# A Fourier convolution with two expert layers on one core: the beginning in another order, with weight pieces on POOL and chunk 3's sums later

## The chip, the core and the metric

The kernel runs on one core of a Trainium2 chip. The metric is the device time of one execution in microseconds, the median of several runs. The engines are called PE (matrix products), DVE and ACT (elementwise), POOL (a second, slower elementwise engine, which also issues DMAs here) and SP (issues DMAs). Each engine works through its own instructions strictly in their order and waits where an operand isn't there.

## The reference, cut to what matters

```python
X = np.fft.rfft(x, axis=1)                       # x: 8 batches, 3072 points, 256 channels
y = np.fft.irfft(X * (filt_r + 1j * filt_i), n=3072, axis=1)
t = y.reshape(8 * 3072, 256)                     # 24576 tokens
h = np.maximum(np.maximum(t @ w1, t @ w2), t @ w3)    # w1, w2, w3: 256 x 768
t = h @ w_out                                    # first expert layer; w_out: 768 x 256
h = t @ w_in                                     # second expert layer, 1024 wide
solu = h * softmax(h)
out = layer_norm(solu) * g_ln @ w_out2
```

## The kernel before, in words

The channels of a batch make two chunks of 128, so there are 16 chunks, numbered batch by batch. A transform of 3072 points is split into 24 times 128. Chunks 0 to 3 (the first two batches) get their 24-point sums on PE, in quarters of 8 small products (`quarter`, L696 to L708 before the change), and after the transform back their parts go to DRAM (`parts_i`). They are read back turned (`turn_in`, into the tile `z`) and get their last sums on PE against the constant `im` (`turn_first`). The later chunks do their 24-point sums on DVE.

`first_batch` does chunks 0 and 1 before everything else, as eight units, a unit being a chunk and one of four groups of frequencies, in the order of `UNITS`. A unit has three stages. `fwd_in`: ACT multiplies the slab `S` by twiddles, DVE sums the products to `U`. `middle`: four PE products of `U` with the constant `dfull`, then on DVE two products with the filter `F` (tiles `Y` and `M2`, read from PSUM) and two sums. `inv_out`: four PE products of `Y`, which ACT copies to `v0` and writes to DRAM. For six units a tile is 384 columns wide, for two (the group `(0, 3)` and `(1, 3)`) 512.

Then the first expert layer begins. Tokens come in tiles of 512, six to a batch, and `moe(i)` is one step of one tile and 128 of the 768 hidden columns, six steps to a tile. `up` makes 12 PE products; ACT and DVE take the maximum and split it into a high and a low part (`hh`, `hl`). `down` is the six products with `w_out`, two steps behind `up` (`LD = 2`), so PE asks for a step's `hl` only after the `up` of the two next steps. `xT` makes the input of a tile. The kernel uses w1 - w3 and w2 - w3 and adds x times A, A being w3 times w_out, at a tile's end.

The weights arrive as float64 bits. `moe_weights` takes them in 12 pieces of 128 by 512 (`PIECES`; for each third of the hidden columns first w3, then w1, w2, w_out). A piece takes five DVE and two ACT operations to become float32 (`from_f64`), then up to three more on DVE and a cast on ACT for the difference, the high and the low part. Ten pieces (`EARLY`) stand among the units, the others behind them. At the end `moe_weights` makes A.

The transforms of chunks 2 to 15 run beside the expert layer. They are one long generator (`fft_stream`), and after each step the main loop lets it advance until its counted DVE work reaches a line set by the step's number (`PACE`, `LEAD`). A scheduler fixes every engine's order when the program is built; `issue_after(x)` keeps instructions behind `x` on x's engine.

Of the kernel before, what the change touches and what calls it, by code (L numbers as in the profile page):

```python
# [10 lines left out]
F32 = mybir.dt.float32  # L11
# [127 lines left out]
def kernel(ctx: ExitStack, tc: tile.TileContext, x0, xr, ff, tw, dft, first_f, first_i,  # L139
# [17 lines left out]
    make_identity(nc, ident)  # L157

# [56 lines left out]
    EARLY = 10  # L215

    def moe_weights():

        raws = yp.tile([P, 3, 1024], I32, tag="s4", name="raws")
        for i, (q, j) in enumerate(PIECES):  # L220
# [13 lines left out]
            with tc.issue_after(GATE[0]) if i >= EARLY else nullcontext():  # L234
                v = from_f64(raw, e, w3f[:, :, fs] if j == 2 else None, nc.vector)
# [4 lines left out]
                if j < 2:  # L240
                    nc.vector.tensor_tensor(v, v, w3f[:, :, fs], op=ALU.subtract)
                nc.scalar.copy(hi, v)
                o = nc.vector.tensor_tensor(lo, v, hi, op=ALU.subtract)
# [3 lines left out]
        pw = [bank() for c in range(2)]  # L247
        for f in range(NF):
# [7 lines left out]
            for c in range(2):  # L256
                cs = slice(c * P, (c + 1) * P)
                nc.tensor.matmul(pw[c][:, :D], th[:, cs], wo_h[:, f], start=f == 0, stop=False)
                nc.tensor.matmul(pw[c][:, :D], tl[:, cs], wo_h[:, f], start=False, stop=False)
                nc.tensor.matmul(pw[c][:, :D], th[:, cs], wo_l[:, f], start=False, stop=f == NF - 1)  # L260
        for c in range(2):
            nc.scalar.copy(a_h[:, c], pw[c][:, :D])
            nc.vector.tensor_tensor(a_l[:, c], pw[c][:, :D], a_h[:, c], op=ALU.subtract)
# [207 lines left out]
    def middle(ch, g):  # L471
# [19 lines left out]
        nc.sync.dma_start(F.rearrange("p r w -> p (r w)"), ff[dc, :, foff:foff + 2 * W])  # L491
# [47 lines left out]
    def inv_out(ch, g):  # L539
# [22 lines left out]
        if ch < 2 * BF:  # L562
# [10 lines left out]
            nc.scalar.dma_start(parts_i[ch][6 * g:6 * g + 6].rearrange("s n d -> n s d"), v)  # L573
# [82 lines left out]
    def fft_stream():  # L656

        last = 2 * B - 1
        yield from groups(2)
# [10 lines left out]
    FZ, SUMS = {}, {}  # L670
# [7 lines left out]
    def first_batch():  # L678
# [16 lines left out]
        def quarter(ch, q, eng):  # L695
            if ch < 2:  # L696
                xs = xa[ch][0][:NT, 8 * q:8 * q + 8] if q < 3 else xa[ch][1][:NT]
            else:
                r = 12 + 8 * (q % 2)
                xs = scr0[:NT, r:r + 8]  # L700
                nc.sync.dma_start(xs, x0[ch, :, 8 * q:8 * q + 8])
            pf = pairbank(0)
# [6 lines left out]

        busy(4)  # L710
        for ch in range(2):
            S[ch] = slab(ch)
            for q in range(4):
                e = quarter(ch, q, nc.scalar if q % 2 and not ch else nc.vector)
                if (ch, q) == (1, 1):
                    behind = e.ins
            for _ in fwd_in(*UNITS[ch]):
                pass
        with tc.issue_after(behind):
            for _ in range(2):  # L720
                next(wgen)
        behind = e.ins
        S[2], S[3] = slab(2), slab(3)
        for i, u in enumerate(UNITS):
# [4 lines left out]
            for q in {0: (0, 1), 2: (2,), 4: (3,)}.get(i, ()):  # L729
                quarter(2, q, nc.scalar)  # L730
            with tc.issue_after(behind):
# [3 lines left out]
                for _ in inv_out(*u):  # L735
                    pass
                if i in (1, 2, 3, 5, 6):
                    next(wgen)
            if i == 4:
                FZ["z"] = fc.tile([P, 2, 2, 6, P], F32, tag="s0", name="z0")  # L740
                turn_in(0, 0, (0,))
            if i == 6:
                FZ["im"] = fc.tile([P, NG, NT], F32, tag="s1", name="im")
                nc.sync.dma_start(FZ["im"][:NT], first_i)
                nc.sync.dma_start(df, dft[:, 0:4])
        GATE.append(behind)
        turn_in(0, 0, (1,))
        with tc.issue_after(FZ["mm"]):
            for q in range(4):
                quarter(3, q, nc.scalar)  # L750
        with tc.issue_after(behind):
            for _ in range(3):
                next(wgen)
# [463 lines left out]
```

## Time and profile before

| | |
|---|---|
| median of 3 runs | 2709.89 us (2709.13 to 2710.82) |
| the profiled execution | 2711.81 us |
| its span in the trace | 2710.0 us |
| PE busy | 2671.7 us, 99% of the span |
| DVE, ACT, POOL busy | 2154.2, 1579.1, 909.1 us |
| mean granted TensorE clock | 0.994 of full speed |

The profile is of one execution; the times in the rows are its own. Busy time of PE counts a product that runs at half the clock as fully busy, so idle time and the granted clock have to be read together. The span is 1.8 us shorter than the profiled execution's own time, and that is 1.9 us above the median.

### The profile page before, as it was taken

The page shows a single profiled execution, that of the slowest core. Times are in us where ns is not written, and L with a number is a line of the kernel's source. Part 1 is how long each engine was busy: PE and PEld are TensorE (multiplying, and loading weights), DVE is VectorE, ACT ScalarE, POOL GpSimd, SP SyncE. Part 2 cuts the span into 40 slices and gives each one's busy share as a digit, 9 for nine tenths or more (in the row PEclk, how much of TensorE's full clock was granted, in tenths as well). Part 3 has the DMA queues.
Part 4 walks back from the last instruction along what each step waited for, and adds up shares of the span by engine and source line. Part 5 has one row for each costly group of instructions (what it writes and reads, how often), then busy time and mean ns, then how long its engine had stood idle before and what let it go on. Part 6 is the DMA issues. An engine that isn't in the chain of part 4 may idle for free.

```text
span 2710.0 us, 38330 instructions
## 1 busy us (share of the span) xinstructions
PE 2671.7 (99%) x12368; PEld 2178.7 (80%) x12368; DVE 2154.2 (79%) x3539; ACT 1579.1 (58%) x3000; POOL 909.1 (34%) x1311
## 2 busy tenths in 40 slices
PE   8899999999999999999999999999999999999999
PEld 6677777877777777777887888888888888888888
DVE  6787787699998999989755447878877887888875
ACT  5544554455555555546344335777777777777775
POOL 0011111011111111121010003767667666767675
PEclk9899999999999999999999999999999999999999
DMA  7633223133223223232123104555555555555553
GB/s 218 189 112 115 75 77 87 63 82 119 68 68 124 74 75 111 75 104 75 47 79 89 37 24 107 150 144 147 149 145 143 140 142 141 141 147 144 142 129 89
DMA packets 168937, 297.17 MB, mean 110 GB/s; under 512 B 33600, under 2 KB 99136, under 8 KB 167104
## 3 DMA queue, kind: packets, MB, share of 16 engines
q1 hardware_dynamic: 113024, 232.77, 32.4%
q10 hardware_dynamic: 54416, 57.24, 6.6%
q0 software_dynamic: 1296, 4.72, 0.5%
q8 instruction: 97, 1.59, 0.3%
q14 instruction: 104, 0.85, 0.1%
HBM read 97.20 MB, written 56.62 MB: 57 GB/s over the span
## 4 chain that ended last, share of the span: by engine, by line
PE 80%; DVE 11%; DMA 4%; issue 2%; SPq 1%; ACT 1%; POOL 1%; DVEq 0%; ACTq 0%; POOLq 0%
PE h L822 21%; PE h L1005 19%; PE p L1074 13%; PE p L1076 7%; PE pf L433 5%; PE o L851 4%; PE o L843 4%; PE o L844 3%; PE o L842 3%; DVE scr L285 2%; DVE S L285 1%; DVE M L285 1%; DMA swap<-M 1%; SPq L782 1%; DVE h L827 1%
## 5 line engine op out<-in xcount | busy, mean ns | idle before, releaser
L1067 POOL TENSOR_TENSOR sl<-zt,sh 128x1024 fp32r<-128x1024 f32 x188 | 453.8, 2414 | 117.5 <-ACT sh L1066 107.5
L1074 PE MATMUL p<-V,sh 128*128 128x512 f32 x1536 | 380.4, 389 | 0.0
L285 POOL TENSOR_TENSOR M<-M,M 128x384 f32<-128x384 f32 (+1 forms) x112 | 153.2, 1389 | 666.2 <-DVE M L285 525.7
L830 ACT CAST hh<-h 128x512 fp32r<-128x512 f32 x288 | 170.6, 592 | 329.9 <-DVE h L827 314.4
L1016 DVE SCALAR_TENSOR_TENSOR sp<-h,e 128x1024 f32<-128x1024 f32 x192 | 234.1, 1219 | 153.1 <-ACT e L1014 151.2
L1074 PEld LDWEIGHTS p<-V,sh 128*128 128x128 f32 x1536 | 287.2, 188 | 59.3
L1014 ACT ACTIVATE e<-h,sm 128x1024 f32<-128x1024 f32 x192 | 213.8, 1114 | 110.3 <-DVE sm L1012 70.4
L825 ACT ACTIVATE hm<-h 128x512 f32<-128x512 f32 x288 | 174.4, 607 | 170.8 <-PE h L822 170.1
L1012 DVE TENSOR_REDUCE sm<-h 128x1 f32<-128x1024 f32 x192 | 231.6, 1206 | 47.8 <-PE h L1005 46.8
L827 DVE TENSOR_TENSOR h<-hm,h 128x512 f32<-128x512 f32 x288 | 197.6, 686 | 79.5 <-PE h L822 77.2
L1066 ACT CAST sh<-zt 128x1024 fp32r<-128x1024 f32 x188 | 196.6, 1047 | 106.8 <-PE p L1074 92.9
L1018 ACT ACTIVATE e<-sp,sm 128x1024 f32<-128x1024 f32 x192 | 220.5, 1148 | 54.4 <-DVE sm L1020 46.5
L1005 PE MATMUL h<-wih,x2h 128*128 128x512 f32 x768 | 242.9, 392 | 1.2 <-ACT xo L854 1.2
L831 DVE TENSOR_TENSOR hl<-h,hh 128x512 fp32r<-128x512 f32 x288 | 196.3, 683 | 58.8 <-ACT hh L830 58.7
L1005 PE MATMUL h<-wih,x2l 128*128 128x512 f32 x768 | 242.1, 391 | 0.0
L843 PE MATMUL o<-hl,woh 128*128 128x512 f32 x576 | 234.9, 408 | 6.4 <-DVE hl L831 6.1
L1005 PE MATMUL h<-wil,x2h 128*128 128x512 f32 x768 | 238.5, 390 | 0.0
L1033 DVE STREAM_TRANSPOSE yt<-sp 128x1024 f32<-128x1024 f32 x188 | 231.5, 1231 | 4.1
L842 PE MATMUL o<-hh,woh 128*128 128x512 f32 x576 | 232.4, 404 | 0.8 <-ACT hh L830 0.8
L844 PE MATMUL o<-hh,wol 128*128 128x512 f32 x576 | 225.9, 392 | 0.0
L1076 PEld LDWEIGHTS p<-V,sl 128*128 128x128 f32 x1536 | 209.7, 190 | 14.9
L1076 PE MATMUL p<-V,sl 128*128 128x256 f32 x1536 | 214.9, 282 | 0.0
(175 smaller groups left out, 5693.2 us busy)
## 6 DMA issues: line engine op xcount, KB each, us to landing
zt<-yt SPq DMA_DIRECT2D x752, 128.0 KB, 2.6
x<-xo SPq DMA_DIRECT2D x96, 256.0 KB, 2.2
x<-x ACTq DMA_DIRECT2D x48, 512.0 KB, 3.6
F<-in_ff_dram SPq DMA_DIRECT2D x48, 384.0 KB, 3.5
S<-in_xr_dram SPq DMA_DIRECT2D x12, 1536.0 KB, 7.2
out_dram<-ob ACTq DMA_DIRECT2D x144, 128.0 KB, 2.3
zt<-yt SPq DMA_DIRECT2D x560, 32.0 KB, 1.8
F<-in_ff_dram SPq DMA_DIRECT2D x16, 512.0 KB, 3.8
```

Source lines behind the costliest of these rows:

```text
L285: return eng.tensor_tensor(o, a, b, op=op)
L822: nc.tensor.matmul(ph[j], wt[:, c, f * P:(f + 1) * P], xt[:, c], start=i == 0, stop=i == 5)
L842: nc.tensor.matmul(po[m], wo_h[:, f, cs], hh, start=f == 0, stop=False)
L843: nc.tensor.matmul(po[m], wo_h[:, f, cs], hl, start=False, stop=False)
L844: nc.tensor.matmul(po[m], wo_l[:, f, cs], hh, start=False, stop=False)
L1005: nc.tensor.matmul(h[:, fs], xt[:, c, ts], wt[:, c, fs], start=n == 0, stop=n == 5)
L1012: nc.vector.tensor_reduce(sm[:, 0:1], h, axis=AX.X, op=ALU.max, negate=True)
L1016: nc.vector.scalar_tensor_tensor(sp, h, 1.0, e, op0=ALU.mult, op1=ALU.mult, accum_out=sm[:, 2:3])
L1033: nc.vector.transpose(out=YT[g][:, :, t].rearrange("p j c k -> p c j k"), in_=sp.rearrange("p (c j k) -> p c j k", c=NF2, j=4))
L1067: nc.gpsimd.tensor_tensor(lv, z, hv, op=ALU.subtract)
L1074: nc.tensor.matmul(p, sh[:, c], V2[:, c], start=c == 0, stop=False)
L1076: nc.tensor.matmul(p[:, :D], sl[:, c], V2[:, c, :D], start=False, stop=c == NF2 - 1)
```

## The change

The line numbers of the changed kernel are higher by 8 in the transforms, by 17 in `quarter` and by 45 or 46 in the expert layer. It does the following.

- The first ten steps take tiles 0 and 1 in turn for the first third of the hidden columns (`BOTH`), and then tile 0, then tile 1. Tile 0 gets its own accumulator (`ob`), whose banks go to the transforms after step 9.
- Six instead of ten weight pieces stand among the units, starting at the third, and of these six the last product, the difference, the cast and the low part go from DVE and ACT to POOL. Six pieces stay behind the units.
- Unit 0's and unit 1's `fwd_in` come before chunk 1's quarters. Chunk 2's quarters come at units 5, 6 and 7 and behind the last unit. Chunk 3's four quarters go into the transform stream (`later`).
- Each unit's parts are read back alone, for tiles 0 and 1, four units later. The last unit's are written in eight pieces by ACT and SP and read back in two halves of the rows.
- The transform stream starts behind step 9 instead of step 4, and its line is five steps later.
- A's two halves share one PSUM bank, which a product with zeros opens.

```diff
-    EARLY = 10
+    EARLY = 6
...
             with tc.issue_after(GATE[0]) if i >= EARLY else nullcontext():
-                v = from_f64(raw, e, w3f[:, :, fs] if j == 2 else None, nc.vector)
+                eng = nc.gpsimd if i < EARLY else nc.vector
+                v = from_f64(raw, e, w3f[:, :, fs] if j == 2 else None, eng)
...
-                nc.scalar.copy(hi, v)
-                o = nc.vector.tensor_tensor(lo, v, hi, op=ALU.subtract)
+                if i < EARLY:
+                    nc.gpsimd.tensor_copy(hi, v)
+                else:
+                    nc.scalar.copy(hi, v)
+                o = eng.tensor_tensor(lo, v, hi, op=ALU.subtract)
...
+            if (ch, g) == UNITS[-1]:
+                for r in (slice(0, 12), slice(12, NG)):
+                    for i in range(NI):
+                        queue = nc.scalar if i % 2 else nc.sync
+                        queue.dma_start(dst[NG * i:NG * (i + 1)][r], v[NG * i:NG * (i + 1)][r])
+                    if not r.start:
+                        turn_in(0, 0, ch, g)
+                        turn_in(0, 1, ch, g)
...
+            if i == 0:
+                quarter(1, 3, nc.vector, first(7))
...
-                for _ in inv_out(*u):
+                for _ in inv_out(*u) if i < 7 else ():
                     pass
-                if i in (1, 2, 3, 5, 6):
-                    next(wgen)
+                if i >= 2 and i < 2 + EARLY:
+                    with tc.issue_after(FL[UNITS[1]]):
+                        next(wgen)
+            if i in (5, 6, 7):
+                quarter(2, i - 5, nc.scalar, x2[:NT, 8 * (i - 5):8 * (i - 5) + 8])
...
+            if i >= 4:
+                turn_in(0, 0, *UNITS[i - 4])
+                turn_in(0, 1, *UNITS[i - 4])
...
         with tc.issue_after(FZ["mm"]):
+            quarter(2, 3, nc.scalar, x23)
...
+        def later():
             for q in range(4):
-                quarter(3, q, nc.scalar)
-        with tc.issue_after(behind):
-            for _ in range(3):
-                next(wgen)
...
+                quarter(3, q, nc.scalar, xs[q])
+                yield
...
-    steps = [(b, tg, f) for b in range(B) for tg in range(TG) for f in range(NF)]
+    BOTH = [(0, 0), (0, 1), (1, 0), (1, 1)] + [(tg, f) for tg in range(2) for f in range(2, NF)]
+    steps = [(0, tg, f) for tg, f in BOTH]
+    steps += [(b, tg, f) for b in range(B) for tg in range(TG) for f in range(NF) if b or tg > 1]
...
-        if i < 4:
-
+        if i < NB:
             continue
...
-        while cost[0] - c0 < (i + 1) * PACE + LEAD * min(1.0, i / RAMP) and idle < 12:
+        while cost[0] - c0 < (i - 4) * PACE + LEAD * min(1.0, (i - 5) / RAMP) and idle < 12:
```

The first place is the first unit on PE. `U` with `dfull` is the unit's first product, `f24` marks a quarter, `Y` the product back. Before:

```order
L705 MATMUL pf_257<-f24_154,xq_164 128x24x4 x8
L433 MATMUL pf_305<-U_216,dfull_137 128x384 x4
L705 MATMUL pf_317<-f24_154,scr0_142 128x24x4 x8
L705 MATMUL pf_328<-f24_154,scr0_142 128x24x4 x8
L433 MATMUL pf_348<-Y_310,dfull_137 128x384
L433 MATMUL pf_358<-U_267,dfull_137 128x384 x4
L433 MATMUL pf_348<-Y_310,dfull_137 128x384 x3
```

With the change:

```order
L722 MATMUL pf_259<-f24_156,xa_165 128x24x4 x8
L441 MATMUL pf_273<-U_219,dfull_139 128x384
L722 MATMUL pf_284<-f24_156,xq_166 128x24x4 x6
L441 MATMUL pf_273<-U_219,dfull_139 128x384 x3
L722 MATMUL pf_284<-f24_156,xq_166 128x24x4 x2
L441 MATMUL pf_304<-Y_278,dfull_139 128x384
L441 MATMUL pf_314<-U_229,dfull_139 128x384 x4
L441 MATMUL pf_304<-Y_278,dfull_139 128x384 x3
```

Two quarters of chunk 2 are gone from between the unit's products and the first product back; only the rest of chunk 1's last quarter stands there.

The second place is the end of `first_batch` on PE, up to the first tile of the expert layer (`h` from `im` and `z`). Before:

```order
L433 MATMUL pf_614<-Y_608,dfull_137 128x384 x3
L433 MATMUL pf_651<-Y_645,dfull_137 128x384 x4
L705 MATMUL pf_661<-f24_154,scr0_142 128x24x4 x8
L705 MATMUL pf_672<-f24_154,scr0_142 128x24x4 x8
L705 MATMUL pf_683<-f24_154,scr0_142 128x24x4 x8
L705 MATMUL pf_694<-f24_154,scr0_142 128x24x4 x8
L767 MATMUL h_751<-im_635,z0_555 128x96 x5
```

With the change:

```order
L722 MATMUL pf_541<-f24_156,x2_269 128x24x4 x8
L441 MATMUL pf_555<-U_460,dfull_139 128x384
L441 MATMUL pf_521<-Y_505,dfull_139 128x384 x3
L441 MATMUL pf_555<-U_460,dfull_139 128x384 x3
L441 MATMUL pf_566<-Y_560,dfull_139 128x384
L722 MATMUL pf_584<-f24_156,x2_269 128x24x4 x8
L441 MATMUL pf_598<-U_511,dfull_139 128x384
L441 MATMUL pf_566<-Y_560,dfull_139 128x384 x3
L441 MATMUL pf_598<-U_511,dfull_139 128x384 x3
L722 MATMUL pf_622<-f24_156,x2_269 128x24x4 x8
L441 MATMUL pf_642<-Y_603,dfull_139 128x384 x4
L722 MATMUL pf_659<-f24_156,scr0_144 128x24x4 x8
```

Chunk 3's four quarters are gone from behind the last product back, and one quarter of chunk 2 (`pf_659`) stands there, right ahead of the first tile; the other quarters of chunk 2 stand among the last units, where `Y_560` follows at once on the products of `U_460` that it depends on.

The third place is DVE between the low parts `hl` of two steps in a row of the expert layer, steps 12 and 13 of the changed kernel, counted from 0. `scr` and `S` are the sums of 24 points of chunk 4, `Z`, `M1` and `U` belong to chunk 2:

```order
L876 TENSOR_TENSOR hl_1552<-h_1535,hh_1551 128x512
L293 TENSOR_TENSOR scr_1346<-S_1344 128x1536 x2
L293 TENSOR_TENSOR scr_1346<-scr_1346 128x768
L293 TENSOR_TENSOR S_1344<-scr_1346 128x768
L293 TENSOR_TENSOR S_1344<-scr_1346 128x384 x2
L873 TENSOR_TENSOR h_1619<-hm_1632,h_1619 128x512
L293 TENSOR_TENSOR scr_1346<-scr_1346 128x384 x2
L297 SCALAR_TENSOR_TENSOR Z_1232<-pf_1227,tws_137,M2_1233 128x768
L297 SCALAR_TENSOR_TENSOR S_1344<-scr_1346 128x768 x2
L293 TENSOR_TENSOR U_1251<-U_1251,T_1252 128x384 x2
L293 TENSOR_TENSOR M1_1240<-Z_1232,F_1225 128x768
L876 TENSOR_TENSOR hl_1636<-h_1619,hh_1635 128x512
```

Before the change such sums of chunk 4 stood between the steps 4 to 8; they have moved about eight steps back, into steps that had little DVE work.

## Rows read from the trace of the kernel before

**Rows 1.** The page: busy us of each engine, share of the span, instructions.
```profile
PE 2671.7 (99%) x12368; PEld 2178.7 (80%) x12368; DVE 2154.2 (79%) x3539; ACT 1579.1 (58%) x3000; POOL 909.1 (34%) x1311
```
**Rows 2.** Windows: stretch, length, busy us (instructions) by engine, PE clock, DMA share, GB/s.
```profile
0.00:89.23 89.23, 76.94 (x330) 49.84 (x330) 64.32 (x111) 49.24 (x106) 6.39 (x15) 0.95 0.80 223
89.23:105.23 16.00, 10.03 (x65) 9.44 (x63) 9.57 (x19) 8.87 (x13) 1.45 (x2) 0.71 0.66 184
105.23:115.00 9.77, 9.77 (x36) 8.69 (x37) 9.66 (x19) 6.45 (x13) 0.00 (x0) 0.56 0.23 60
115.00:150.00 35.00, 33.08 (x159) 25.51 (x158) 24.04 (x37) 21.32 (x52) 6.54 (x7) 1.00 0.58 175
150.00:170.00 20.00, 15.46 (x64) 11.17 (x63) 19.01 (x26) 7.79 (x17) 3.18 (x2) 0.91 0.39 113
170.00:1600.00 1430.00, 1421.42 (x6130) 1131.78 (x6129) 1166.09 (x1730) 712.84 (x1582) 167.64 (x137) 1.00 0.28 81
1600.00:2710.00 1110.00, 1104.97 (x5595) 942.31 (x5593) 861.49 (x1601) 772.63 (x1221) 723.88 (x1148) 1.00 0.52 134
```
**Rows 3.** PE's timeline: start, us, instruction, records; in brackets idle before it and releaser.
```profile
25.79 3.85 PE L705 MATMUL pf<-f,scr 96*128 96x96 f32 x32 [1.53 <-DMA scr<-in_x_dram]
...
31.13 2.74 PE L433 MATMUL pf<-U,dfull 128*128 128x384 f32 x8
33.71 2.10 PE L433 MATMUL pf<-Y,dfull 128*128 128x384 f32 x6
...
52.34 2.01 PE L433 MATMUL pf<-Y,dfull 128*128 128x512 f32 x2 [2.41 <-DVE Y L285]
...
83.77 5.46 PE L433 MATMUL pf<-Y,dfull 128*128 128x384 f32 x8 [3.02 <-DVE Y L285]
...
105.23 5.33 PE L767 MATMUL h<-im,z 96*128 96x96 f32 x24 [0.89 <-ACT S L708]
...
169.48 0.40 PE L844 MATMUL o<-hh,wol 128*128 128x512 f32 x1
169.71 0.39 PE L842 MATMUL o<-hh,woh 128*128 128x512 f32 x1
```
**Rows 4.** DVE's timeline in one unit, with weight operations between.
```profile
40.29 0.95 DVE L285 TENSOR_TENSOR Y<-pf,F 128x768 f32<-128x768 f32 x1
41.16 0.95 DVE L285 TENSOR_TENSOR M<-pf,F 128x768 f32<-128x768 f32 x1
42.02 0.42 DVE L201 TENSOR_SCALAR raws<-raws 128x512 int32<-128x512 int32 x1
42.35 1.02 DVE L285 TENSOR_TENSOR Y<-Y,M 128x384 f32<-128x384 f32 x2
43.29 0.68 DVE L285 TENSOR_TENSOR U<-U,T 128x512 f32<-128x512 f32 x1
43.90 0.42 DVE L197 TENSOR_SCALAR we<-raws 128x512 int32<-128x512 int32 x1
```
**Rows 5.** ACT's timeline: the last unit's copy.
```profile
89.27 0.80 ACT L566 COPY v<-pf 128x768 f32<-128x768 f32 x1 [2.20 <-PE pf L433]
```
**Rows 6.** The tile of the parts in DRAM: its writes, from issue to landing.
```profile
DMA to landing us min/median/max: 2.7/3.5/12.1
```
**Rows 7.** The tile of the parts read back, from issue to landing.
```profile
DMA to landing us min/median/max: 2.9/3.4/10.0
```
**Rows 8.** Groups by shape on POOL: count, busy us, mean ns, idle before and releasers.
```profile
L208 POOL TENSOR_TENSOR we<-we,raw 128x512 f32<-128x512 f32 x8 | 10.7, 1347 | 121.0 <-DVE raw L203 119.0 <-POOL we L208 2.0
```
**Rows 9.** POOL's timeline: the same pair of operations twice.
```profile
196.60 2.97 POOL L285 TENSOR_TENSOR M<-M,M 128x384 f32<-128x384 f32 x2 [0.94 <-DVE M L285]
...
277.78 1.96 POOL L285 TENSOR_TENSOR M<-M,M 128x384 f32<-128x384 f32 x2 [8.45 <-DVE M L285]
```
**Rows 10.** DVE's timeline: the same pair of sums twice.
```profile
170.91 2.08 DVE L285 TENSOR_TENSOR scr<-S 128x1024 f32<-128x1024 f32 x2
...
197.44 2.95 DVE L285 TENSOR_TENSOR scr<-S 128x1024 f32<-128x1024 f32 x2
```

More of the change, by code (lines that the diff above doesn't have):

```diff
@@ L246, in moe_weights @@
             yield
-        pw = [bank() for c in range(2)]
+        t = bank()
+        pw = [t[:, c * D:(c + 1) * D] for c in range(2)]
+        nc.tensor.matmul(t, zeros, w_h[0][:, 0, :512], start=True, stop=False)
         for f in range(NF):
@@ L658, in fft_stream @@
         last = 2 * B - 1
-        yield from groups(2)
+        yield from together(groups(2), FZ["later"])
         yield from together(groups(3, rest(2)), stages(None, 4))
@@ L708, in quarter, with first @@
             return nc.scalar.copy(to, src) if eng is nc.scalar else nc.vector.tensor_copy(to, src)
+        def first(q):
+            return xa[q // 4][0][:NT, 8 * (q % 4):8 * (q % 4) + 8] if q % 4 < 3 else xa[q // 4][1][:NT]
         busy(4)
[L711 to L717, printed above, removed]
-                pass
-        with tc.issue_after(behind):
-            for _ in range(2):
-                next(wgen)
-        behind = e.ins
-        S[2], S[3] = slab(2), slab(3)
+        S[0], S[1] = slab(0), slab(1)
+        for q in range(4):
+            e = quarter(0, q, nc.scalar if q % 2 else nc.vector, first(q))
+        behind = e.ins
+        for u in UNITS[:2]:
+            for _ in fwd_in(*u):
+                pass
+        for q in range(3):
+            quarter(1, q, nc.vector, first(4 + q))
+        x2 = fc.tile([P, 24, P], F32, tag="s3", name="x2")
+        S[2] = slab(2)
         for i, u in enumerate(UNITS):
@@ L728, in first_batch @@
             behind = SUMS[u]
-            for q in {0: (0, 1), 2: (2,), 4: (3,)}.get(i, ()):
-                quarter(2, q, nc.scalar)
+            if i == 0:
+                quarter(1, 3, nc.vector, first(7))
+            if i == 2:
+                with tc.issue_after(FL[u]):
+                    for q in range(3):
+                        nc.sync.dma_start(x2[:NT, 8 * q:8 * q + 8], x0[2, :, 8 * q:8 * q + 8])
             with tc.issue_after(behind):
@@ L746, in first_batch @@
         GATE.append(behind)
[L747 removed]
+        with tc.issue_after(behind):
+            for _ in inv_out(*UNITS[7]):
+                pass
         with tc.issue_after(FZ["mm"]):
[L749 to L755 removed]
+            quarter(2, 3, nc.scalar, x23)
+        S[3] = slab(3)
+        with tc.issue_after(FZ["in"]):
+            nc.sync.dma_start(FZ["im"][:NT, 12:], first_i[:, 12:])
+            nc.sync.dma_start(df, dft[:, 0:4])
+            xs = [staged(3, q) for q in range(2)]
@@ L875, in moe @@
         j = b * TG + tg + 1
+        if j == 1:
+            if f == 0:
+                xT(0, 1)
+            return
         if f == XF and j < B * TG:
```

83 lines of the change are left out of this document (50 added, 33 removed).

## The prediction

> **What bounds the kernel now.** I read the page first: PE is busy for 2671.7 of 2710.0 us [rows 1], so the kernel is bound by PE, and no change that leaves PE its products can win more than PE's idle time of 38.3 us and what a low clock costs. The windows then say where these lie [rows 2]. Idle, length less PE busy: 12.3 us until 89.23 (the end of the eighth unit's last product), 6.0 to 105.23 (the first tile's first sums), nothing to 115, 1.9 to 150, 4.5 to 170; behind that 8.6 and 5.0 in 2540 us. Busy time at a low clock, busy times (1 - clock): 3.8 us until 89.23, 2.9, 4.3, 0 and 1.4 in the next four windows. So 24.7 us of idle time and about 12.4 us of clock lie before 170 us, and the change is made there. The reader is to see in the timeline of PE what idles do: after 1.53 us without work 32 records took 3.85 us, after 2.41 us two records took 2.01 us, and after 3.02 us eight took 5.46 us, where eight of the same shape take 2.74 elsewhere [rows 3]. The last is the lower of the clock's two levels, 1.2 instead of 2.4 GHz.
>
> **The change, up to the eighth unit's end.** PE's products stay the same but for one with zeros (0.23 us, the spacing of two 512-column products in [rows 3]), so I add work at full clock and idle time. Work until 89.23 is 76.9 less 3.8 for the clock, 73.1 us. Chunk 2's last quarter moves behind it: two quarters take 3.85 us [rows 3], one 1.9. Left are 71.2 us.
>
> Idle time comes from a chain. From the end of a unit's products to its first product back DVE does two products with the filter and one sum: 0.87 + 0.87 + 0.47 = 2.2 us by the starts in [rows 4] (the pair of sums takes 0.94). For the two wide units I take 1.04 per 1024 columns from [rows 10] and 0.6 for 512 from [rows 4], about 2.8. Meanwhile PE has three products of the unit before, 2.10 us [rows 3]. Weight operations of DVE came on top of the chain before the change; now a piece costs DVE five operations (0.34 each where one operand is read, 0.61 where two are [rows 4], 2.2 us) instead of up to eight, and they mostly fit between the chains. So I walk along the new order of PE: the start as before 1.9; the first unit, with only the rest of a quarter as cover, 2.7; the next two 0.25 each; the wide ones 0.9 and, with a weight operation in front of the sum, 1.35; the sixth 0.8; the seventh 2.3, because chunk 2's quarter stands ahead of `U_460`'s last products and nothing is left behind them; the eighth 1.0. That is 11.5 us against 12.3 before: the stalls are made up of other pieces, and few are gone. The end would come at 71.2 + 11.5 = 82.7.
>
> Two things are added. **The clock**: idles of 2.7 and 2.3 us may each cost between nothing and the 2.7 us that the one of 3.02 cost [rows 3], 0 to 5.4 together; I take 2.5, near the middle, since 2.41 cost about 2 with what followed. **POOL**: it now does 17 operations for the six pieces. The nearest row is 1.35 us for a product of that size [rows 8]; the casts have no row, and I give them the same, with nothing as the other bound. That is 23 us in a stretch where it did 6.4 us, and the last piece is wanted only by the fifth step, some 19 us behind the first tile, so POOL itself is in time. But at 196.60 a pair of POOL took 2.97 us that takes 1.96 elsewhere [rows 9], and just then a pair of sums on DVE took 2.95 instead of 2.08 [rows 10]: both slow down, DVE by 0.87 in 2.97 us. At that rate 23 us of POOL cost DVE 6.7 us at most, and nothing at least. The operations of the chain that read two tiles of SBUF are the sums, about a quarter of it; I take 1.5. By the Trainium skill (GPSIMD Engine Reference, section Specifications) POOL shares its SBUF interfaces with VectorE and contends with DVE instructions that have two SBUF inputs or run in a two-port mode; the trace agrees, as the two pairs show. If that held for all of POOL's new work, the full 6.7 us would stand in the sum. So the eighth unit ends at 86.7.
>
> **From there to the first tile.** The last parts take a copy on ACT of 0.8 us [rows 5], a write of 2.7 to 3.5 [rows 6] and a read of 2.9 to 3.4 us [rows 7], 6.4 to 7.7; I take 7.0, as the pieces are smaller but SP issues four writes before the read. (The medians count; the longest landings lie where the DMA engines are full.) One quarter covers 1.9 of it, the first tile starts at 93.7, and the clock falls again as it did before. Before it started at 105.23, but with chunk 3's four quarters done, 7.7 us, which PE now pays later. Gain: 105.2 - 7.7 - 93.7 = **3.8 us**.
>
> **Behind it.** The slow clock at the first tile cost 4.3 us (9.77 at 0.56 [rows 2]) and I leave it. What goes are the idle times of 1.9 and 4.5 us and 1.4 us of clock to 170 [rows 2], 7.9 together: there DVE had the last weights, A and chunk 4's sums at once (busy 19.0 of 20 us). In the new order the first ten steps hold no transforms. From the first tile to step 7, DVE's 53 rows come to 28.6 us (14 at 0.34, 39 at 0.61), and PE's to 35 (two tiles of first sums at 2.7, eight times twelve products and six times six at 0.23), so PE sets the pace; 0 to 4 us may remain at A, whose parts go round PE, ACT and DVE, and I take 1.5. Gain **6.4 us**. The pieces that wait for a free raw buffer and POOL's DMA lie inside DVE's margin of 7 us.
>
> **Later.** The transforms are late: priced by width from [rows 4], DVE's rows of the stream stand 53 us behind at step 12, 5 behind at step 64, and level at the end. This work comes into steps where DVE has room: it was busy for 1166 of 1430 us [rows 2]. But the new order is dense in steps 13 to 19, with 48 us of DVE against 37 of PE; the place shown above between two `hl` alone is some 12 us (1.6 for 1536 columns by the rate of [rows 10], 768 and 384 by [rows 4]). PE asks for an `hl` two steps late, which covers about 13 us there. Idle time behind 170 is 13.6 us now; I expect **1.5 us** more (between 3 less and 9 more).
>
> **Sum.** 3.8 + 6.4 - 1.5 = 8.7 us off the profiled execution's own 2711.8, 2703.1; the median of the runs is 1.9 us lower, so about 2701.
>
> **The rivals.** *The stalls go altogether*: neither idle lets the clock fall, POOL costs nothing, and A's round trips hide. That is 2.5 + 1.5 + 1.5, and 3 later: 2693. For it: idles below 1.6 us left the clock alone. Against it: 2.41 did not. Chance 0.15. *POOL takes back what DVE loses*: the 6.7 us instead of 1.5 gives 2706, within the bound; the pairs speak for it, that most of the chain reads PSUM against it. Chance 0.15. (The page named above, GPSIMD Engine Reference of the Trainium skill, states this sharing as a rule.) *The change does not shorten the way to the first tile*: the parts read back singly share SP with the filter's loads and cost a landing of 10 or 12 us [rows 6, 7] once, so the gain of 3.8 turns to a loss of about 1: 2706. The DMA engines are at 0.66 then, and a full queue is not seen. Chance 0.12. *The slower side: the late transforms come due.* In four places the new order has more DVE than PE work (steps 13 to 19, 44 to 48, 76 to 80, 88 to 92: 10.7, 7.6, 6.6 and 8.3 us more, 33 in all); the old order's five densest have 15. If waits for DMAs in the transforms use up the two steps of cover, up to 18 us more than now stand as idle: 2719. It decides from 14 us. Against it: DVE has room on both sides of each place. Chance 0.10.
>
> **Numbers.** The forecast has 0.48: 2701, by its own bounds 2696 to 2704. A measurement of this kernel can tell 0.2%, 5.4 us. Faster by more (under 2704.5): forecast and stalls gone, 0.63. Within: the two at 2706, 0.27. Slower: 0.10. The range goes from 2692 to 2709, which leaves out the slower side and the far end of the stalls gone.
>
> **What would show it.** Right: an idle of 2 to 3 us at the first and the seventh unit, the eighth unit's last product ending at 84 to 89, the first tile at 91 to 97, no idle above 1.5 us in the first ten steps but at A, and chunk 3's quarters between later steps at full clock. Wrong: sums of a unit that take well over 0.94 us while POOL works; a longer landing ahead of the first tile; PE waiting for `hl` in steps 13 to 25; or PE's idle time behind 250 us above 20 us.

## The result, and the profile after

The changed kernel takes 2740.9 us (median of 4 runs, 2739.8 to 2743.1), the kernel before 2709.5 in the same comparison: 1.0117 times as long, 95% interval 1.0099 to 1.0134. It is slower by 31.4 us, where I had forecast 2701, 8.7 us less; the range ended at 2709.

PE's windows in the kernel after show where the time went. They are cut at the eighth unit's last product (98.59), around the start of the steps, and around the end of batch 0; columns as in [rows 2].

```profile
0.00:98.59 98.59, 81.88 (x314) 52.26 (x315) 58.84 (x90) 41.04 (x89) 20.92 (x26) 0.88 0.62 178
98.59:115.00 16.41, 11.62 (x60) 10.27 (x59) 8.65 (x13) 5.25 (x8) 5.87 (x6) 0.67 0.82 215
115.00:150.00 35.00, 32.16 (x140) 25.40 (x139) 28.25 (x51) 21.42 (x41) 1.45 (x2) 0.96 0.34 107
150.00:170.00 20.00, 19.92 (x108) 17.23 (x108) 7.86 (x16) 9.40 (x21) 0.00 (x0) 1.00 0.05 19
170.00:300.00 130.00, 129.10 (x626) 104.87 (x625) 94.41 (x129) 59.61 (x125) 14.16 (x12) 1.00 0.36 107
300.00:350.00 50.00, 35.54 (x130) 24.41 (x129) 28.98 (x41) 17.70 (x40) 7.77 (x6) 0.83 0.37 105
350.00:1600.00 1250.00, 1238.29 (x5271) 980.44 (x5271) 1056.54 (x1573) 637.93 (x1434) 158.08 (x128) 1.00 0.28 82
1600.00:2741.30 1141.30, 1135.97 (x5731) 968.15 (x5730) 873.51 (x1618) 784.79 (x1242) 724.32 (x1148) 1.00 0.51 132
```

Two places stand out. Up to the eighth unit's end there are 16.7 us of idle time and 81.88 x 0.12 = 9.8 us lost to the clock, 9.4 us later than before [rows 2]. And in 300 to 350, 14.5 us are idle and 35.54 x 0.17 = 6.0 go to the clock, 20.5 us together. From 150 to 170, where 4.5 us were idle [rows 2], there are 0.08. In the kernel before nothing was lost between 300 and 350:

```profile
300.00:350.00 50.00, 50.00 (x219) 38.99 (x218) 44.36 (x65) 27.63 (x68) 7.09 (x5) 1.00 0.22 61
```

PE's timeline of the first place: `Y` of a unit is what its first product back waits for. After the idle time of 4.16 us the granted clock is about half (0.52 from 67.65 to 77.30, the lower of its two levels) until about 77: six records take 3.70 us, where others take 2.10.

```profile
26.82 1.62 PE L441 MATMUL pf<-Y,dfull 128*128 128x384 f32 x2 [2.92 <-DVE Y L293]
...
39.05 2.10 PE L441 MATMUL pf<-Y,dfull 128*128 128x384 f32 x6
...
57.66 1.10 PE L441 MATMUL pf<-Y,dfull 128*128 128x512 f32 x2 [1.59 <-DVE Y L293]
...
67.65 1.62 PE L441 MATMUL pf<-Y,dfull 128*128 128x384 f32 x2 [4.16 <-DVE Y L293]
73.75 3.70 PE L441 MATMUL pf<-Y,dfull 128*128 128x384 f32 x6
81.99 0.88 PE L441 MATMUL pf<-Y,dfull 128*128 128x384 f32 x2 [2.60 <-DVE Y L293]
...
93.91 4.68 PE L441 MATMUL pf<-Y,dfull 128*128 128x384 f32 x8 [1.31 <-DVE Y L293]
102.42 1.52 PE L813 MATMUL h<-im,z 96*128 96x96 f32 x12 [2.07 <-ACT S L725]
```

DVE's and POOL's timeline just ahead of the 4.16 us. A pair of sums of this size took 1.29 us at 48.55, and a pair of `U` 1.02 at 49.76; here they lie beside POOL's operations and take 2.37 and 2.95.

```profile
48.55 1.29 DVE L293 TENSOR_TENSOR Y<-Y,M 128x512 f32<-128x512 f32 x2
49.76 1.02 DVE L293 TENSOR_TENSOR U<-U,T 128x384 f32<-128x384 f32 x2
...
56.83 2.37 DVE L293 TENSOR_TENSOR Y<-Y,M 128x512 f32<-128x512 f32 x2
57.00 1.65 POOL L210 TENSOR_TENSOR we<-we,raws 128x512 f32<-128x512 f32 x1 [8.34 <-DVE raws L205]
58.73 1.60 POOL L244 TENSOR_TENSOR we<-we,scr 128x512 f32<-128x512 f32 x1
59.13 2.95 DVE L293 TENSOR_TENSOR U<-U,T 128x384 f32<-128x384 f32 x2
```

PE's timeline of the second place, and ahead of it the uses of the stream's one tile of PSUM (`pf`, pool `ps_f`). It is opened when tile 0's accumulator is free. Chunk 3's quarters come first, 6 to 7 us from one to the next, and chunk 2's first unit only at 199.42 (before at 114). At 327 PE has run out of steps of batch 0 and waits: for a unit of chunk 3, and for its parts to be read back.

```profile
172.14 1.95 PE L722 MATMUL pf<-f,scr 96*128 96x96 f32 x16
178.28 1.92 PE L722 MATMUL pf<-f,scr 96*128 96x96 f32 x16
185.33 1.92 PE L722 MATMUL pf<-f,scr 96*128 96x96 f32 x16
192.37 1.92 PE L722 MATMUL pf<-f,scr 96*128 96x96 f32 x16
199.42 1.45 PE L441 MATMUL pf<-U,df 128*128 128x384 f32 x4
...
325.40 1.56 PE L441 MATMUL pf<-EO,df 128*128 128x384 f32 x4
334.98 3.33 PE L441 MATMUL pf<-EO,df 128*128 128x512 f32 x4 [8.02 <-DVE EO L297]
339.85 2.93 PE L441 MATMUL pf<-U,df 128*128 128x384 f32 x4 [1.55 <-DVE v L297]
346.62 2.77 PE L813 MATMUL h<-im,z 96*128 96x96 f32 x12 [3.85 <-DMA z<-pi]
```

`EO`, which the 8.02 us wait for, is the input of a unit's second use of the tile. DVE makes it from `swap`, and it waited for the DMA that fills `swap`:

```profile
334.08 0.75 DVE L297 SCALAR_TENSOR_TENSOR EO<-swap,tws,M 128x512 f32<-128x512 f32 x1 [4.51 <-DMA swap<-M]
```

### The profile page after: what moved, and what is told of

Same layout as the page of the kernel before. It is cut to its first block, busy times and chain, and to the rows that moved or that the text cites. A ratio compares the mean times of both kernels' runs of the same rounds, so it can differ in the third digit from the quotient of the medians.

```text
span 2741.3 us, 38400 instructions
## 1 busy us (share of the span) xinstructions
PE 2684.5 (98%) x12369; PEld 2183.0 (80%) x12369; DVE 2157.0 (79%) x3527; ACT 1577.1 (58%) x2996; POOL 932.6 (34%) x1328
## 3 DMA queue, kind: packets, MB, share of 16 engines
q8 instruction: 97, 1.59, 0.3%
## 4 chain that ended last, share of the span: by engine, by line
PE 84%; DVE 9%; DMA 3%; issue 2%; SPq 1%; ACT 1%; POOL 0%; DVEq 0%; ACTq 0%; POOLq 0%
PE h L868 22%; PE h L1062 19%; PE p L1131 13%; PE p L1133 7%; PE pf L441 6%; PE o L896 4%; PE o L888 4%; PE o L889 4%; PE o L887 4%; DVE scr L293 2%; DVE S L293 1%; PE pf L722 1%; DVE S L297 1%; DVE hl L876 1%; DVE h L873 1%
## 6 DMA issues: line engine op xcount, KB each, us to landing
zt<-yt SPq DMA_DIRECT2D x752, 128.0 KB
out_dram<-ob ACTq DMA_DIRECT2D x144, 128.0 KB
```

## The experiments

Each time is a median; the ratio is to the kernel before on the same chip, with its 95% interval.

| run | what | us | ratio |
|---|---|---|---|
| e1 | after, old line | 2741.3 | 1.0118 (1.0103 to 1.0133) |
| e2 | after, early pieces on DVE, ACT | 2736.2 | 1.0098 (1.0083 to 1.0113) |
| e3 | after, chunk 3's quarters first | 2735.2 | 1.0096 (1.0081 to 1.0111) |
| e4 | before, late start and line | 2715.7 | 1.0024 (1.0013 to 1.0035) |
| e5 | after, quarters in the steps' banks | 2722.2 | 1.0043 (1.0028 to 1.0059) |
| e6 | after, POOL does the casts only | 2738.2 | 1.0103 (1.0089 to 1.0117) |
| e7 | before, tiles in turn | 2711.5 | 1.0009 (1.0000 to 1.0018) |
| e8 | e5 and e2 together | 2719.6 | 1.0040 (1.0026 to 1.0053) |
| e9 | before, 21 products on POOL | 2720.5 | 1.0039 (1.0024 to 1.0055) |
| e10 | before, 42 copies on POOL | 2728.5 | one run |
| e11 | after, quarters behind chunk 2 | 2742.1 | 1.0122 (1.0107 to 1.0136) |
| e12 | e7, earlier loads | 2708.4 | 0.9991 (0.9982 to 1.0000) |
| e13 | before, quarters in the stream | 2707.2 | 0.9991 (0.9981 to 1.0000) |
| e14 | e7, quarters in the stream | 2728.2 | 1.0066 (1.0051 to 1.0081) |
| e15 | e7, quarters in the steps' banks | 2712.4 | 1.0015 (1.0006 to 1.0024) |
| e16 | e15, chunk 1 read by unit | 2712.3 | 1.0013 (1.0004 to 1.0022) |

**The stall at the end of batch 0: e1, e3, e4, e5.**

```diff
# e1
-        while cost[0] - c0 < (i - 4) * PACE + LEAD * min(1.0, (i - 5) / RAMP) and idle < 12:
+        while cost[0] - c0 < (i + 1) * PACE + LEAD * min(1.0, i / RAMP) and idle < 12:
# e3: in first_batch, in place of the generator later()
+        with tc.issue_after(FZ["mm"]):
+            for q in range(4):
+                quarter(3, q, nc.scalar, xs[q])
...
# e4 (before)
-        if i < 4:
+        if i < 9:            # and the line of after
# e5: a quarter of chunk 3 in two of the steps' tiles; in the main loop
+        if i in (1, 3, 5, 7):
+            next(FZ["later"])
...
```

> The kernel after, but the due line of the stream behind the ninth step is the old one, which is some 15,400 units (five steps' worth) further on; the start stays at the tenth step. In the trace of after PE stands idle for 14.5 us and at a lower clock between 300 and 350 us, where batch 0 ends and the first tile of batch 1 wants chunk 3's last units. Theory 1 (the stream is simply late: started at step 9 on a line that lies five steps lower): the idle time at the end of batch 0 goes, PE's busy time in 300 to 350 comes to about 49 us, and the time falls by some 18 to 22 us, to 2719 to 2723. Theory 2 (chunk 3's four quarters, which now stand ahead of chunk 2's first unit in the stream and go one by one through a single tile of PSUM, hold chunk 2's units back by some 30 us, whatever the line asks for): most of the idle time stays, and the time is 2732 or more. The beginning before 150 us is as in after under both.

e1 settles nothing: the scheduler puts the instructions of PE, DVE and POOL in the same order as in after, so the run is after once more. The number in the code that looks like the stream's pace doesn't bind here.

> The kernel after, but chunk 3's four quarters are done ahead of the first tile, as before the change, instead of as the first four items of the stream. Theory 2 (the quarters in the stream, on one tile of PSUM, are what makes chunk 3's last units late at the end of batch 0): chunk 2's first unit runs some 20 to 30 us earlier than in after (at 202), PE's idle time between 300 and 350 us falls from 14.5 us to under 4, and the time falls by about 15 to 20 us, to 2721 to 2726; the quarters' 7.7 us of PE are only moved, and part of them fills the wait ahead of the first tile. Theory 1 (the later line alone): the idle time there stays at 10 us or more, and the time is 2733 to 2743.

Between 300 and 350 PE is busy for 50.00 us, as theory 2 says, but that decides little. The quarters now stand ahead of the first tile, and PE waits 12.67 us for the loads of their x there, so the first tile starts at 132.9 instead of 102.4. Chunk 2's first unit is hardly earlier, at 197.8 instead of 199.4; it is the deadline that came 30 us later. The gain is only 5.7 us.

> The kernel before, with one part of the change: the stream of transforms starts behind the ninth step instead of the fourth, on the line that lies five steps lower. Start, order of the tiles, weight pieces and chunk 3's quarters are those of before. Theory 1 (lateness of the stream by itself starves the end of batch 0): PE stands idle for 8 to 15 us where batch 0 ends, and the time rises by 8 to 20 us, to 2718 to 2730. Theory 2 (only together with chunk 3's quarters in the stream): idle time there under 3 us, and the time is 2705 to 2713.

e4 doesn't test what it was made for: chunk 2's first unit is where it was (its first DVE operation at 117.6 us, 116.8 in before), since only a gate on the weights was lost. 6.4 us are idle in 150 to 200 (4.5 before), where A and the transforms meet, and the time fits neither theory. The next run decides.

> The kernel after, but chunk 3's four quarters take two of the four tiles of PSUM that the steps use, and stand between the first ten steps instead of at the head of the stream. Theory 2 (the four round trips of the quarters through the one tile of the stream make chunk 3's last units late at the end of batch 0): chunk 2's first unit, which ran at 202 us in after, runs at about 175 to 180, PE's idle time between 300 and 350 us falls from 14.5 to under 4 us with the clock at 0.97 or more, and the time falls by 14 to 20 us, to 2721 to 2727. Rival (the lateness comes from starting the stream behind ten steps, and the quarters have little to do with it): the idle time at the end of batch 0 stays above 8 us and the time above 2731. The beginning up to 100 us is that of after under both.

It does: 18.7 us less than after, and the stall is gone. PE's window in e5:

```profile
300.00:350.00 50.00, 49.50 (x219) 39.08 (x219) 33.12 (x47) 27.14 (x64) 6.94 (x7) 1.00 0.35 100
```

Chunk 2's first product with `U` came at 181.9, later than I said, and still early enough.

**Place in the chain, or its length: e11, e13, e14.**

```diff
# e11 (after)
-        yield from together(groups(2), FZ["later"])
+        yield from groups(2)
+        yield from FZ["later"]
# e13 (before) and e14 (e7): first_batch leaves chunk 3's quarters to later()
-        yield from groups(2)
+        yield from together(groups(2), FZ["later"])
```

> The kernel after, but chunk 3's quarters stay in the stream and on its one tile of PSUM, and come behind chunk 2's units instead of ahead of them. Theory 2a (they stand at the head of the stream, each waiting for a load of x, the products and a copy, while nothing else may use the tile): chunk 2's first unit runs at about 175 us instead of 202, the quarters' waits hide between the other units' transforms, and the time is 2721 to 2730 with under 6 us of idle time at the end of batch 0. Theory 2b (what counts is the length of the whole chain through the one tile of PSUM, quarters included, wherever they stand in it): the idle time at the end of batch 0 stays at 10 us or more, and the time is above 2733.

> The kernel before, with chunk 3's four quarters as items of the stream instead of ahead of the first tile; everything else, the stream's start behind the fourth step too, is that of before. By the chain (start at 114 us, four quarters of 7 us, sixteen uses of the tile at 8.2 us: 273 us, some 45 us ahead of where the tile of before was done with chunk 3) nothing starves at the end of batch 0: idle time under 2 us between 300 and 350 us, and the time is 2704 to 2714, of which the first tile's wait is the uncertain part. If quarters in the stream starve the end of batch 0 whatever the start, 5 to 15 us of idle time stand there and the time is above 2718.

> The run with the two tiles in turn and the beginning of before (2711.5 us, no idle time between 300 and 350), with chunk 3's four quarters as items of the stream. By the chain (start near 166 us, four quarters of 7 us, sixteen uses of the tile at 8.2 us: 325 us, and 10 us more for the write and the read, against the last step of batch 0 at about 320 to 325 us) PE stands idle for 6 to 16 us where batch 0 ends, and the time is 2720 to 2734. If the late start and the quarters cost nothing together without the new beginning and POOL's work, the idle time there is under 3 us and the time is 2706 to 2714.

PE's windows in e11, e13 and e14, one after the other:

```profile
300.00:350.00 50.00, 33.74 (x122) 22.54 (x121) 31.00 (x45) 18.36 (x39) 7.11 (x6) 0.80 0.41 116
```
```profile
300.00:350.00 50.00, 50.00 (x221) 39.38 (x220) 41.15 (x63) 29.86 (x73) 9.00 (x7) 1.00 0.29 82
```
```profile
300.00:350.00 50.00, 32.91 (x123) 23.73 (x123) 22.01 (x32) 18.87 (x46) 6.67 (x7) 0.83 0.37 100
```

It is the length. In e11 chunk 2 starts at 173.0, and the quarters take their 29.6 us behind three of its units: the stall is as long as in after. With the early start of before (e13) the same quarters in the stream cost nothing; with the late one (e14) they bring the stall back, 17.1 us of idle time, without POOL's work and with the old beginning. The chain, read off PE's timelines as starts of the uses of `pf` (us; 16 uses for chunks 2 and 3, from the first to the start of the last):

| run | first use | quarters | 16 uses | last one | PE out of steps |
|---|---|---|---|---|---|
| after | 172.1 | 27.3 | 135.6 | 335.0 | 327.0 |
| e14 | 159.8 | 27.3 | 133.7 | 320.8 | 312.8 |
| e5 | 181.9 | none | 131.6 | 313.5 | never |
| e7 | 168.5 | none | 128.0 | 296.5 | never |

What sets the pace of this chain is not shown. A use follows the last one after 8.5 to 9.0 us on average, but in after the tile is in use, from a first product to the last reading by ACT or DVE, for only 82 of the 135.6 us and for 11 of the quarters' 27.3. Between its two uses each unit also sends its tiles through `swap` by DMA, and the last wait was for such a DMA. No run gave the stream a second tile.

**POOL: e2, e6, e8, e9, e10.**

```diff
# e2 (e6 keeps the cast on POOL)
-                eng = nc.gpsimd if i < EARLY else nc.vector
+                eng = nc.vector
...
-                    nc.gpsimd.tensor_copy(hi, v)
+                    nc.scalar.copy(hi, v)
# e9 (before), behind a unit's sums; e10 has six tensor_copy(idle, M1[:, 0, :384])
+            if (ch, g) != UNITS[-1]:
+                for _ in range(3):
+                    nc.gpsimd.tensor_tensor(FZ["idle"], M1[:, 0, :384], M1[:, 1, :384], op=ALU.mult)
```

> The kernel after, but the early weight pieces do their subtractions on DVE and their casts on ACT, as all pieces did before the change. Theory C (contention: POOL's new work slows DVE's sums and the weight operations, and the idle times of PE and its low clock in the first 100 us follow from that): no pair of sums of a wide unit takes above 2.1 us, those of a unit of 384 columns 1.0 to 1.3, the eighth unit's last product ends at about 88 to 91 instead of 98.5, and the time falls by 6 to 9 us, to 2732 to 2735. Rival (the chain from a unit's products over DVE's filter products and sums back to its first product back is uncovered because of the new order of quarters and units, with POOL a bystander): DVE gets some 12 us of work more in the same stretch, the eighth unit ends at 96 to 102, and the time is within 4 us of after's 2741.

The mechanism is that of theory C, the sizes lie a little outside it: the eighth unit ends at 91.8 instead of 98.6, and 4.7 us of it reach the end. On the same chip e1, the same program as after, took 2740.5 to 2742.0 us and e2 2732.5 to 2738.2. In e2's DVE timeline the two pairs are back, and in PE's the 4.16 us are 1.59:

```profile
57.37 1.29 DVE L290 TENSOR_TENSOR Y<-Y,M 128x512 f32<-128x512 f32 x2
58.58 1.02 DVE L290 TENSOR_TENSOR U<-U,T 128x384 f32<-128x384 f32 x2
```
```profile
65.62 0.88 PE L438 MATMUL pf<-Y,dfull 128*128 128x384 f32 x2 [1.59 <-DVE Y L290]
...
75.95 1.62 PE L438 MATMUL pf<-Y,dfull 128*128 128x384 f32 x2 [3.15 <-DVE Y L290]
...
88.98 2.82 PE L438 MATMUL pf<-Y,dfull 128*128 128x384 f32 x8 [0.84 <-ACT S L722]
```

> The kernel after, but of the early weight pieces only the cast is left to POOL; their subtractions and products with two operands in SBUF are DVE's, as before the change. Theory C as it stands after the run with everything back on DVE and ACT (it is POOL's operations with two operands, 1.27 to 1.67 us each, that stretch DVE's pairs from 1.29 and 1.02 to 2.37 and 2.95 us; casts of 0.6 us do not): no pair of sums above 1.4 us, the eighth unit's last product ends at 91 to 93, and the time is 2734 to 2738, as with everything back. Rival (any work of POOL on SBUF disturbs DVE): pairs that meet a cast are stretched to 1.6 us or more, the eighth unit ends at 94 or later, and the time is 2738 to 2742.

The eighth unit ends at 89.3, one pair beside a cast takes 1.43; the time lies between the two theories and tells little.

> The two repairs together: chunk 3's quarters between the first ten steps in the steps' own tiles of PSUM, and the early weight pieces back on DVE and ACT. If the two causes are separate (quarters at the head of the stream; POOL slowing DVE), their gains add: 14 to 20 and 4.7 us off after's 2741, 2716 to 2722, and what is left over the kernel before is the idle time and the low clock of the first 100 us from the new order of quarters and units. If they overlap (the stream's chain is what sets the end of batch 0, so that an earlier first tile gives nothing), the time is that of the repair of the quarters alone, within 2 us.

On top of e5 the repair gives 2.6 us at the end, though the eighth unit ends 8.9 us earlier (88.7 against 97.6). The runs of the two overlap (2718.1 to 2725.4 and 2720.1 to 2723.7), so whether the gains add is not decided; what the beginning gains does not all reach the end.

> The kernel before, with the suspected cost by itself: behind the sums of each of the first seven units POOL does three products of 128x384 of that unit's two halves into a tile that nobody reads, 21 in all. The order of the instructions on PE, DVE and ACT is that of before, row for row. Theory C (POOL's operations with two operands in SBUF stretch DVE's, whoever needs them): the products of POOL take about 1.0 us alone; DVE's sums of two operands that meet them take 1.5 to 2.9 us a pair instead of 1.02 to 1.29, the eighth unit's last product ends 3 to 8 us later than at 89.2, and the time is 2711 to 2717. Rival (the long pairs in the trace of after came from something else, and POOL is a bystander): pairs as before, within 0.1 us, and the time is 2706 to 2711.

The order on PE, DVE and ACT is that of before; the eighth unit ends at 93.3 (before 89.2), and the time is 10.3 us above before's. That is more than I said, and not all contention: twice DVE also waits for POOL to have read a `Y` (1.31 and 1.46 us), which the experiment brought in. Two pairs of `U` are stretched from 1.02 to 1.82; the other pairs keep their time, and there operations with one operand, or POOL's products, take longer. DVE's and POOL's rows:

```profile
45.36 3.59 POOL L509 TENSOR_TENSOR idle<-Y 128x384 f32<-128x384 f32 x3 [3.07 <-DVE Y L285]
45.73 1.23 DVE L197 TENSOR_SCALAR we<-raws 128x512 int32<-128x512 int32 x1
46.88 1.22 DVE L199 TENSOR_SCALAR raws<-raws 128x512 int32<-128x512 int32 x1
...
56.36 1.02 DVE L285 TENSOR_TENSOR U<-U,T 128x384 f32<-128x384 f32 x2
56.60 5.72 POOL L509 TENSOR_TENSOR idle<-Y 128x384 f32<-128x384 f32 x3 [5.07 <-DVE Y L285]
...
68.03 1.82 DVE L285 TENSOR_TENSOR U<-U,T 128x384 f32<-128x384 f32 x2
68.27 3.52 POOL L509 TENSOR_TENSOR idle<-Y 128x384 f32<-128x384 f32 x3
```

> As the run with two operands, but six copies of 128x384 with one operand behind each of the first seven units, 42 in all, so that POOL works for about as long. Here the order on PE and DVE changes a little as well, so the durations are what is read, not the time. If only POOL's operations with two operands in SBUF disturb DVE, DVE's pairs of sums stay at 1.02 and 1.29 us also where a copy runs beside them; if any work of POOL in SBUF does, pairs beside copies take 1.3 us or more.

The first half is refuted. A copy with one operand stretches pairs of sums too; the product with the filter, which reads PSUM, keeps its 1.22:

```profile
53.48 1.22 DVE L285 TENSOR_TENSOR M<-pf,F 128x1024 f32<-128x1024 f32 x1
53.70 4.58 POOL L509 COPY idle<-Y 128x384 f32<-128x384 f32 x6
...
55.24 1.89 DVE L285 TENSOR_TENSOR Y<-Y,M 128x512 f32<-128x512 f32 x2
...
57.06 1.63 DVE L285 TENSOR_TENSOR U<-U,T 128x384 f32<-128x384 f32 x2
```

**The good part by itself: e7, e12, e15, e16.** e7 is the kernel before with `BOTH`, the `ob` tile, A's sums in one bank and the start behind step 9.

```diff
# e12: loads of chunk 3's x
+            if i in (3, 5):
+                XS[3, i // 4] = staged(3, i // 4)
# e15: as e5, on e7.  e16: behind units 5 to 7
+                for tg in range(2):
+                    turn_in(0, tg, (1,), UNITS[i - 1][1])
```

> The kernel before, with one part of the change: the first steps take the two tiles in turn, the stream starts behind the ninth step on the lower line, and A's sums take one bank. The order of quarters and units up to the first tile, the weight pieces on DVE and ACT, the reading back by chunk, and chunk 3's quarters ahead of the first tile are those of before. If my prediction's second part is right (behind the first tile the idle times of 1.9 and 4.5 us and 1.4 us of clock until 170 go, 6.4 of gain, and lateness costs 1.5 later), PE stands idle for under 2 us from 120 to 200, there is no idle time above 3 us at the end of batch 0, and the time is 2700 to 2706. If lateness alone starves the end of batch 0 once ten steps come first, 5 to 15 us of idle time stand between 300 and 350 and the time is 2710 to 2722.

> The kernel of the run with the two tiles in turn and the beginning of before, with one thing more: the loads of chunk 3's first two quarters are issued two units earlier, since PE waited 2.38 us for the first of them ahead of the first tile and then ran at the lower clock (32 records in 6.96 us). If that wait is on the way to the first tile, the quarters end 2 to 4 us earlier and the time falls from 2711.5 to 2707 to 2710, below that of before by at most 0.1 per cent. If the read of the last parts sets the first tile anyway, nothing changes within 2 us.

> The beginning of before (order of quarters and units, weight pieces on DVE and ACT, reading back by chunk), the two tiles in turn, and chunk 3's quarters between the first ten steps in the steps' own tiles of PSUM. From e14 (2728.2 us) the stall at the end of batch 0 should go, 17 us of idle time and 5.6 us of clock: about 2706. If the gain survives to the end, 2703 to 2708; if the later waits for hl take it back as they did in e7, 2709 to 2714.

> As e15, and chunk 1's parts are read back unit by unit, as in the change, so that only the last unit's read follows the last product. In e14 PE stood for 7.74 us until that read had landed. If the size and the number of rows of that last read set the wait, it falls to 3 to 5 us and the time is 3 to 5 us below e15's; if a landing costs the same for 24 rows as for 96 [rows 7], nothing changes within 2 us.

In e7 0.34 us are idle from 120 to 200 and nothing at the end of batch 0, so the first half of its expectation holds; but the time is 2711.5. PE's windows until 200 and from 500 to 1200 in before, e7 and e15, one after the other:

```profile
0.00:200.00 200.00, 175.28 (x785) 128.71 (x786) 155.46 (x249) 107.32 (x231) 20.73 (x29) 0.92 0.59 169
...
500.00:1200.00 700.00, 695.68 (x2922) 546.50 (x2922) 665.19 (x970) 381.64 (x881) 90.45 (x70) 1.00 0.30 88
```
```profile
0.00:200.00 200.00, 183.55 (x838) 140.23 (x839) 143.55 (x235) 100.98 (x210) 13.29 (x22) 0.92 0.53 154
...
500.00:1200.00 700.00, 691.54 (x2883) 542.97 (x2882) 664.53 (x969) 379.98 (x878) 99.88 (x72) 0.99 0.30 88
```
```profile
0.00:200.00 200.00, 177.37 (x847) 135.10 (x848) 144.79 (x237) 101.35 (x213) 13.29 (x22) 0.97 0.52 154
...
500.00:1200.00 700.00, 687.89 (x2879) 540.14 (x2878) 660.80 (x967) 376.65 (x872) 102.86 (x70) 1.00 0.30 87
```

Until 200 us e7 has 8.3 us less idle time than before, but DVE has done 11.9 us less work. From 500 to 1200 DVE is busy for 94 to 95% of the time in all three, and PE's idle time grows from 4.3 to 8.5 and 12.1 us, mostly in waits for `hl` (3.41 us at 530 in e7), with a lower clock behind some. That DVE's late work is what takes the gain back is read from these rows and not tested by a run of its own. e12 waits 2.21 instead of 2.38 us for the load, and the first tile is no earlier; its 3 us against e7 are less than the spread of e7's own runs (2706.3 to 2714.8). e15 and e16 move the wait to the read-back and end together: reading by unit shortens the wait from 8.21 to 6.55 us, not to 3 to 5, and the time does not change. No version here beats the kernel before by a measurable amount.

## Why the prediction was wrong

**The step that failed is "Later", 1.5 us more (between 3 less and 9 more): it measured 20.5 us at the end of batch 0 alone.** I compared DVE's rows with PE's work, step by step, and looked for dense places. The bound was another: chunks 2 and 3 must be finished before batch 1's first tile. Their quarters and units follow one another in one chain, which takes as long wherever the quarters stand in it (e11), and which can begin only when tile 0's accumulator gives its banks to the stream's tile. 172 + 27 + 136 = 335, and the read-back 12 more, against 327. Either part alone starved nothing there (e5, e13), the pair did (e14). My rival on the slower side had the lateness right but the place wrong (an `hl` in steps 13 to 19) and ended at 2719; as its 18 us stand in place of the 1.5, it should be 2717.5. Of my signs of being wrong two came: sums far above 0.94 us beside POOL, and 31.5 us of idle time behind 250.

**POOL's 1.5 us measured 6.8** at the eighth unit's end (e2 against after). The bound of 6.7 that I worked out from [rows 9, 10] as DVE's loss was about right for DVE, which lost some 6.1 us there (three pairs and two operations with one operand). That PE lost nearly the same is luck, for its loss has another make-up: 1.9 us more idle time (16.7 against 14.8) and the rest, 4.9, clock. Two stretched pairs made one idle time of 4.16 us out of 1.59, and more than 9 us at the lower clock followed. The sums are a quarter of the chain, but one of them in the wrong place is enough. By the Trainium skill (Perfetto Trace Analysis, section Optimizing Scalar/DVE Operations) moving work between DVE and POOL might not help, since they share a read port; e2 agrees, with 4.7 us gained by moving it back; the port itself no run here shows.

**The other terms up to the eighth unit.** Work 72.1 us (71.2 forecast). Idle time without POOL 14.8 instead of 11.5: the first wide, the sixth and the seventh unit waited 1.93, 1.59 and 3.15 (0.9, 0.8 and 2.3). Clock 9.8 instead of 2.5, of which POOL's 4.9. Together 98.6 instead of 86.7.

**Nearly right: the way to the first tile.** In after the first tile starts 3.8 us behind the eighth unit's last product, but with the 12 products of chunk 0; those of chunk 1, which need the last parts, start at 104.65, 6.1 us behind it, where I had 7.0. **Half right: the 6.4 us behind it.** The ten steps remove the idle time at A (0.08 us from 150 to 170), and in e7, with the weight pieces of before, only 0.35 us are idle from the first tile to 170. But in after six weight pieces instead of two are still converted behind the units, and from 100 to 150 PE waits 3.1 us for `xl` and 1.2 for `hh`. DVE stood 4.69 us for the load of a weight piece just ahead of one `xl` (4.29 in e2); I had put these loads inside DVE's margin of 7 us. Idle time from the first tile to 170 is 5.6 us against 6.5. (PE's work there up to step 7 was added up to 35 us; the terms give 35.8. Nothing hangs on it.)

**The sum.** The first tile comes 4.9 us later than before less the 7.7 us of quarters (102.4 against 97.5; 3.8 earlier forecast), behind it 1.4 are gained in idle time and clock (6.4 forecast), 20.5 are lost at the end of batch 0, 0.9 from 170 to 300, and 3.4 more idle time stands behind 350 (1.5 forecast for these three): 28 of 31 us. The rest is within the rounding of the clock in the long windows.

**By the runs** 18.7 us belong to the quarters in the late stream (e5) and about 5 to POOL (e2), of which on top of e5 2.6 were measured and not clear of the spread (e8). The 7.2 us between e8 and e15 belong to the new beginning: order of quarters and units, weight pieces, last unit's writes and read-back. They weren't taken apart; e16 speaks only for the read-back by unit, which changed nothing.

## What to carry to other kernels

When work is moved behind other work, look for its deadline and follow the chain that it makes: first use, number of uses and time for each told e14's stall before it ran (the last use foreseen at 325, measured at 320.8). No engine's busy share shows it: DVE was busy for 94 of the 130 us from 170 to 300. A price on an engine that feeds a chain is not the price on PE: slow products behind a longer idle time can cost more than the idle time (here 4.9 us behind 1.9). And idle time removed early only counts if no engine is behind later: ask what the engine that did less meanwhile still has to do.

## What the runs showed of the hardware

DVE's and POOL's operations on tiles in SBUF lengthened each other, in both directions and unevenly. DVE's operation with one operand (128x512, 0.42 us) took 1.22 to 1.49 beside POOL's products, pairs of sums of 1.02 up to 2.95; but at 56.60 in e9 the pair kept 1.02 and POOL's three products took 5.72, where one alone takes 1.01. Copies on POOL with one operand stretch pairs as well (1.63 and 1.89). Products of DVE that read PSUM kept their time (1.22 or 1.23 for 1024 columns, in after and e10). A cast of 128x512 on POOL takes 0.60 us, half of a product (1.27). The Trainium skill (GPSIMD Engine Reference, section Specifications) names DVE's instructions with two SBUF inputs or in a two-port mode as those that contend; the rows of the pairs agree. Whether the stretched operations with one operand run in such a mode no run here shows.
